# Two tiles of the first expert moved among the last operations of attention, with that expert's weights split there

## The chip, the cores and the metric

The kernel runs on one core of one Trainium2 chip. The metric is the device time of one execution in microseconds (us), the median of several runs. A core has five engines with a queue of instructions each: TensorE (PE in the rows, its weight loads PEld), VectorE (DVE), ScalarE (ACT), GpSimd (POOL) and SyncE (SP), which here issues DMAs. An engine takes its queue in order, and the queue is fixed when the kernel is built. An instruction that waits for another engine holds up everything behind it on its own engine.

## The reference

```python
def reference(q,k,v,mem_k,mem_v, moe weights, moe2 weights):   # 4 x 8 heads x 768 x 64
    for each chunk of 32 positions:                            # windowed attention, 8 memory keys
        scores = scale*q_c @ concat(mem_k, k[window]).T
        out_c  = softmax(scores) @ concat(mem_v, v[window])
    x = attention output as (3072, 512)
    # first MoE, one expert of 8 per token
    e = argmax(x @ w_gate);  g = softmax(x @ w_gate)[e] * sigmoid(x @ w_output_gate)[e]
    x = g * (relu(x @ w1[e]) @ w2[e])                          # 512 -> 1024 -> 512
    # second MoE, two experts of 8 per token, noisy logits
    return sum over the top 2 of weight * (relu(x @ w1[e]) @ w2[e])
```

With the inputs of the reference the first MoE's experts get 529, 195, 426, 381, 565, 320, 162 and 494 of the 3072 tokens (counted from the reference's own logits). In tiles of 128 tokens that is 5, 2, 4, 3, 5, 3, 2 and 4: 28 tiles, as many as `SPLIT1`, so the slots behind 28 are not run. Of the first 2304 tokens (18 row tiles of 128) 273 belong to expert 0, which is more than two tiles of it.

## The kernel before

**Attention** has 32 units: 4 batches, 2 halves, 4 pairs of heads. A unit runs S (scores, PE), max and subtraction (DVE), A (transposes, PE), exponentials (ACT), X (weights times values, PE) and the division (DVE, lines 242 to 244). After units 7, 15, 23, 27 and 31 `gating` runs for the finished row tiles (table `GATE`, three row tiles per half): it splits each row into two 16 bit halves with a scale (`parts`), stores the rows to `xrow` in DRAM, computes the logits, the expert and the rank of each token within its expert, and adds the token's place to `acc`, a histogram in PSUM, by a matmul of two one-hot tiles A and B (lines 346 to 348). `acc` says for each expert and rank which token stands there.

All of attention is given as operations with engine, estimated duration, reads and writes and a priority to a planner (`Plan`, lines 149 to 184). It simulates the engines by these estimates and emits the operation that can start first; among those within 60 ns the lowest priority number goes first. The result is a fixed order on each engine.

**Between** stands `placed` (lines 448 to 484): from `acc` and the counts in `base` it works out which tile slot holds which tokens. Line 453 reads `acc`, lines 455 to 457 get the first tile's rows early by an indirect DMA, line 476 writes the experts' first slots as integers, line 478 loads these into DVE registers, line 480 copies seven stretches of `acc` to their slots, and `rows_of` (lines 428 to 436) makes row numbers (`idx`) of all.

**The first MoE** (`moe`, lines 621 to 740) runs over the slots. For a tile: 8 groups of 12 matmuls for h (line 697), relu on ACT (hh, line 698), remainder on DVE (hl, line 699), and 24 matmuls for y (line 735). Then DVE works out a power of two scale (lines 765 to 775), ACT and DVE split y into two halves (`post`, lines 780 and 781), and SP stores the row and transposes it by DMA to x2T (`t2`) for the second MoE's logits, which PE computes two tiles later (`logits`, line 794). Weights are split into high and low halves: w1h and w2h on ACT, w1l and w2l on DVE (`first_w1`, `first_w2h`, `first_w2l`, lines 599 to 614). In the kernel before this is done behind `placed`, in memory that is opened only when attention's pools are closed. The first tile is transposed on PE (`first_trans`, lines 742 to 749), the others by DMA. The second MoE has 51 tiles.

## Time and profile before

| | us |
|---|---|
| median of 3 runs (1101.01 to 1102.67) | 1102.05 |
| the profiled execution | 1104.43 |
| its span in the trace | 1102.5 |
| PE busy | 1009.4 |
| DVE busy | 587.2 |
| ACT busy | 413.5 |
| POOL busy | 268.1 |

The profiled execution is one run and is 2.4 us above the median. Its span begins with the first instruction of the trace; all times of day in the rows are counted from there. The granted clock of PE is given as a share of full speed: 1.0 is 2.4 GHz and 0.5 is 1.2 GHz.

### The profile page before, as it was taken

The numbers are of one execution on the slowest core, as the hardware profiler recorded it, in microseconds if no ns is written. First come the engines' busy times: TensorE is split into PE (matmuls) and PEld (weight loads), VectorE is DVE, ScalarE is ACT, GpSimd is POOL, SyncE is SP. The second block draws the span as 40 slices with busy tenths as digits, with TensorE's granted clock in tenths as the row PEclk, the third lists the DMA queues.
The fourth block names the chain that finished last, engine by engine and source line by source line (L and its number), as shares of the span: only waits on it lengthen the run. The fifth ranks groups of instructions, "written<-read, shape, count | busy, mean of one in ns | idle before, by whom it ended". The sixth has DMA issues, their size and how long they took to land. (4 is left out here: it accounts for less than half of the span.)

```text
span 1102.5 us, 33444 instructions
## 1 busy us (share of the span) xinstructions
PE 1009.4 (92%) x12480; PEld 880.8 (80%) x12480; DVE 587.2 (53%) x1777; ACT 413.5 (38%) x659; POOL 268.1 (24%) x371
## 2 busy tenths in 40 slices
PE   5688839999989999898999999899999999999995
PEld 3567728888878888787888888788888888888884
DVE  3579885376577577858635225335352442525321
ACT  2568862374344365616114114124142331424010
POOL 4434111011111111110123322324233243333321
PEclk7799869999999999999999999999999999999998
DMA  8696229989596969865356537637456374563421
GB/s 324 242 397 229 85 73 260 220 256 307 113 252 148 202 192 191 244 176 141 119 115 180 167 95 150 174 89 194 139 148 192 96 221 138 155 188 84 110 70 35
DMA packets 183575, 190.47 MB, mean 173 GB/s; under 512 B 120378, under 2 KB 139066, under 8 KB 182336
## 3 DMA queue, kind: packets, MB, share of 16 engines
q1 hardware_dynamic: 167904, 139.51, 47.2%
q0 software_dynamic: 14400, 46.27, 14.1%
q8 instruction: 101, 1.65, 0.6%
q10 hardware_dynamic: 1056, 2.10, 0.5%
q14 instruction: 114, 0.93, 0.3%
HBM read 389.51 MB, written 34.53 MB: 385 GB/s over the span
## 5 line engine op out<-in xcount | busy, mean ns | idle before, releaser
L697 PE MATMUL h<-xT,w1h 128*128 128x128 f16 x4928 | 376.4, 219 | 0.0
L697 PEld LDWEIGHTS <-w1h 128*128 128x128 f16 x5056 | 309.3, 98 | 22.9 <-issue 20.7
L698 ACT ACTIVATE hh<-h 128x512 fp32r<-128x512 f32 x158 | 94.2, 597 | 529.4 <-PE h L697 500.4
L699 DVE SCALAR_TENSOR_TENSOR hl<-h,hh 128x512 fp32r<-128x512 f32 x158 | 108.7, 689 | 278.1 <-ACTq L659 180.7
L697 PE MATMUL h<-xT,w1l 128*128 128x128 f16 x2464 | 239.3, 219 | 4.9 <-DVEq L657 3.1
L697 PEld LDWEIGHTS <-w1l 128*128 128x128 f16 x2528 | 169.0, 98 | 7.4 <-DVEq L657 3.2
L933 POOL DMA_INDIRECT out_dram<-o,idxC x51 | 51.3, 1006 | 207.2 <-DVE c L920 187.0
L916 POOL DMA_INDIRECT prev<-out_dram,idxC x50 | 60.7, 1213 | 144.3 <-issue 52.8
L735 PE MATMUL y<-w2h,hl 128*128 128x512 f32 x320 | 86.8, 393 | 4.7 <-DVEq L657 2.8
L735 PE MATMUL y<-w2h,hh 128*128 128x512 f32 x320 | 85.9, 407 | 4.7 <-ACTq L657 3.0
L735 PE MATMUL z<-w2h,hh 128*128 128x512 f32 x312 | 84.4, 412 | 3.7 <-ACT hh L698 2.2
L735 PE MATMUL y<-w2l,hh 128*128 128x512 f32 x320 | 87.1, 395 | 0.0
L735 PE MATMUL z<-w2h,hl 128*128 128x512 f32 x312 | 85.7, 397 | 0.6 <-DVEq L657 0.3
L735 PE MATMUL z<-w2l,hh 128*128 128x512 f32 x312 | 84.6, 393 | 0.0
L596 DVE SCALAR_TENSOR_TENSOR w1l<-stg,wscl,w1h 128x1024 f16<-128x1024 f32 x60 | 74.3, 1279 | 11.7 <-ACT w1h L595 11.7
L614 DVE TENSOR_TENSOR w2l<-stg,w2h 128x1024 fp32r<-128x1024 f32 x64 | 75.4, 1218 | 0.3 <-ACT w2h L618 0.3
L735 PEld LDWEIGHTS y<-w2h,hl 128*128 128x128 f32 x320 | 59.7, 188 | 19.5 <-DVEq L657 3.8
L577 ACT ACTIVATE junk<-stg 128x1024 bf16<-128x1024 f32 x64 | 67.7, 1058 | 16.6 <-DMA stg<-in_w_dram 6.6
L735 PEld LDWEIGHTS z<-w2h,hl 128*128 128x128 f32 x312 | 59.4, 191 | 15.0 <-DVEq L657 1.9
L735 PEld LDWEIGHTS y<-w2l,hh 128*128 128x128 f32 x320 | 60.5, 189 | 13.3
L735 PEld LDWEIGHTS y<-w2h,hh 128*128 128x128 f32 x320 | 55.6, 188 | 19.0 <-ACTq L657 6.0
L618 ACT ACTIVATE w2h<-stg 128x1024 fp32r<-128x1024 f32 x60 | 60.0, 1049 | 28.3 <-PE h L697 14.4
(280 smaller groups left out, 1164.4 us busy)
## 6 DMA issues: line engine op xcount, KB each, us to landing
stg<-in_w_dram SPq DMA_DIRECT2D x312, 1024.0 KB
vx<-in_v_dram SPq DMA_DIRECT2D x8, 1560.0 KB
x<-row SPq DMA_DIRECT2D x26, 256.0 KB
xrow<-rows SPq DMA_DIRECT2D x8, 792.0 KB
out_dram<-zero SPq DMA_DIRECT2D x8, 768.0 KB
qs<-in_q_dram SPq DMA_DIRECT2D x7, 768.0 KB
kk<-in_k_dram SPq DMA_DIRECT2D x4, 800.0 KB
kk<-in_k_dram SPq DMA_DIRECT2D x3, 784.0 KB
```

Source lines behind the costliest of these rows:

```text
L577: for k in range(4): tc.nc.scalar.activation(g.junk,g.stg1[k//2][:,k%2],AF.Abs,accum_out=g.wscl[:,5+k:6+k])
L596: if 1 in parts: nc.vector.scalar_tensor_tensor(l[:,f:f+2],w,g.wscl[:,4:5],h[:,f:f+2],op0=ALU.mult,op1=ALU.subtract)
L614: tc.nc.vector.tensor_tensor(g.w2l[f],quarter(g,f),g.w2h[f],op=ALU.subtract)
L618: tc.nc.scalar.activation(g.w2h[f],quarter(g,f),AF.Copy)
L697: nc.tensor.matmul(o,w[i][:,k,fi%4*128:fi%4*128+128],xt[:,l*4+k],start=n==0,stop=n==11); n+=1
L698: nc.scalar.activation(hh[i],ph[i],AF.Relu)
L699: nc.vector.scalar_tensor_tensor(hl[i],ph[i],0.0,hh[i],op0=ALU.max,op1=ALU.subtract)
L735: for k in range(4): nc.tensor.matmul(py,x[h][:,k],w[2*h+k//2][:,k%2],start=i==0 and k==0,stop=i==5 and k==3)
L916: nc.gpsimd.indirect_dma_start(out=pv[s%2],out_offset=None,in_=out,in_offset=bass.IndirectOffsetOnAxis(ap=ic[s][:,0:1],axis=0), bounds_che ...
L933: nc.gpsimd.indirect_dma_start(out=out,out_offset=bass.IndirectOffsetOnAxis(ap=ic.pop(s)[:,0:1],axis=0),in_=o,in_offset=None, bounds_check ...
```

## The change

`Q1=2` tiles of expert 0 leave the loop over slots and become operations of attention's planner.

- `places`, after unit 23: raises expert 0's count to at least 256, reads the first two columns of `acc` (so only the tokens of the 18 row tiles counted by then), makes their row numbers and gathers both tiles' rows.
- `weights`: splits expert 0's weights with priorities 38 to 40, and loads the second expert's weights after that. Their memory is a pool that takes the place of buffers of attention (`early1`: q, k, v and row buffers of one parity; `early3`: qbd and e), closed as soon as the last units no longer use them.
- `early(t)`: a whole tile with priority 44 or 46, in attention's PSUM tiles A, S and X: 8 transposes, copy, h, hh and hl, y, scales, the split, store and transposing DMA.
- `placed` no longer fetches a first tile. The loop begins at slot 2, with `first_trans` for that slot. `post` and `t2` are not called for slots 0 and 1, the zero fills go to slots 2 to 9, and `tail` is cleared by POOL at the start instead of by DVE in `placed`. `NS1` is 33 instead of 31, and codes for flags are 8192 instead of 4096.

```diff
+    def places():
+        P({"DVE":80},lambda _: nc.vector.tensor_scalar(g.base[:,0:1],g.base[:,0:1],128.0*Q1,None,op0=ALU.max),w=["base"],prio=26.0)
+        def rows(_):
+            nc.vector.tensor_copy(pl,g.acc[:,0:Q1])
+            rows_of(nc,pl,o,idx)
+        P({"DVE":800},rows,w=["idx0"],r=["acc"],prio=26.0)
+        for i in range(Q1):
+            P({"Pool":1300},lambda _,i=i: nc.gpsimd.indirect_dma_start(out=g.x0[i],out_offset=None,in_=g.xrow[0:18*128],
...
+    def weights():
+        P({"SP":1},lambda _: g.room1(),w=["free"]+[("v",0,h) for h in range(2)]+[(a,0,p) for a in ("q","k","kx") for p in range(4)]+[("km",0)]+
+            [("xr",i,p) for i in range(2) for p in range(4)],prio=24.0)
...
+        for half in range(2):
+            for f in (0,2):
+                P({"ACT":940},lambda _,w=w,half=half,f=f: nc.scalar.activation(g.w1h[half][:,f:f+2],w,AF.Copy,scale=g.wscl[:,4:5]),w=[("w1h",half,f)],r=["free","wscl",("stg",f//2)],prio=38+half)
+                P({"DVE":1280},lambda _,w=w,half=half,f=f: nc.vector.scalar_tensor_tensor(g.w1l[half][:,f:f+2],w,g.wscl[:,4:5],g.w1h[half][:,f:f+2],op0=ALU.mult,op1=ALU.subtract),
...
+        for f in range(4):
+            P({"ACT":940},lambda _,f=f: nc.scalar.activation(g.w2h[f],quarter(g,f),AF.Copy),w=[("w2h",f)],r=["free",("stg",2+f//2)],prio=40)
+            P({"DVE":1180},lambda _,f=f: first_w2l(tc,g,f),w=[("w2l",f)],r=[("w2h",f),("stg",2+f//2)],prio=40)
...
+        for c in range(4):
+            P({"ACT":940},lambda _,c=c: nc.scalar.activation(g.junk,g.stg1[c//2][:,c%2],AF.Abs,accum_out=g.wscl[:,5+c:6+c]),w=[("scl2",c)],r=[("stg",c//2)],prio=40.0)
+    def early(t):
+        pr=44.0+2*t
+        def tr(_):
+            for j in range(8): nc.tensor.transpose(pt[:,j],xh[:,j*128:(j+1)*128],g.idh)
+        P({"PE":600},tr,w=["A"],r=[("x0",t),"consts"],prio=pr)
+        P({"ACT":1000},lambda _: nc.scalar.activation(g.xt0_[t],pt,AF.Copy),w=[("xt",t)],r=["A","free"],prio=pr)
+        for i in range(2):
+            for fi in range(4):
...
+                P({"PE":670},mm,w=[("S",i)],r=[("xt",t)]+[(w,i,f) for w in ("w1h","w1l") for f in (0,2)],prio=pr)
+            P({"ACT":600},lambda _,i=i,ph=ph: nc.scalar.activation(hh(i),ph,AF.Relu),w=[("hh",i)],r=[("S",i),"freex"],prio=pr)
+            P({"DVE":660},lambda _,i=i,ph=ph: nc.vector.scalar_tensor_tensor(hl(i),ph,0.0,hh(i),op0=ALU.max,op1=ALU.subtract),w=[("hl",i)],r=[("S",i),("hh",i)],prio=pr)
...
+            P({"PE":930},mm,w=[("X",t)],r=[(("hh","hl")[a],h)]+[(("w2h","w2l")[w],2*h+j) for j in range(2)],prio=pr)
...
+        P({"DVE":1150},scales,w=[("c0",t)],r=[("X",t),("x0",t),"winv"],prio=pr)
...
+        P({"SP":2000},store,r=[("r2",t,0),("r2",t,1)],prio=pr)
...
+        if n==23: places()
...
+    weights()
+    for t in range(Q1): early(t)
     P.run()
...
-    if x0 is not None:
-        o=rt.tile([128,4,1],F32,name="plc0",bufs=1); idx=rt.tile([128,1],I32,name="idx0",bufs=1)
-        rows_of(nc,pl[:,0:1],o,idx)
-        nc.gpsimd.indirect_dma_start(out=x0,out_offset=None,in_=rows,in_offset=bass.IndirectOffsetOnAxis(ap=idx[:,0:1],axis=0))
...
+    if s0==Q1: XT[s0]=first_trans(tc,g,XG[s0])
+    for s in range(s0,s0+2): trans(s)
+    if s0==Q1: tab=tab()
...
-    run(0,SPLIT1,hook_last,tab)
+    run(Q1,SPLIT1,hook_last,tab)
...
-    first_w1(tc,g); first_w2h(tc,g)
-    for f in range(2): first_w2l(tc,g,f)
-    stage1(tc,g,g.w1[1:2])
```

The planner's choices show in the order of instructions. First VectorE where the low halves of w1 are made. Before, all four stand behind `placed`, in a row with the clearing of `tail`:

```order
474 L1003 MEMSET tail 128x496
475 L1004 COPY tail<-plc_2551 128x31 [waits DVE_49]
476 L1011 MEMSET base 128x8
477 L605 SCALAR_TENSOR_TENSOR w1l_2587<-stg_68,wscl,w1h_2585 128x1024 [waits DMAHW6_49,DMAHW5_49,DMAHW7_49,DMAHW4_49,Activation_49]
478 L605 SCALAR_TENSOR_TENSOR w1l_2587<-stg_69,wscl,w1h_2585 128x1024 [waits Activation_49]
```

Now the first of them stands between steps of units 27 and 28 (S, m, e and xr are a unit's tiles, s its sums); three more follow in the next 17 rows and the four of w2 in the 42 after those:

```order
352 L228 MEMSET S_148 64x8 [waits PE_49]
353 L229 TENSOR_REDUCE m_136<-S_148 128x6 [waits DVE_49]
354 L246 TENSOR_SCALAR s_139<-X_152 128x6 [waits PE_49]
355 L385 SCALAR_TENSOR_TENSOR w1l_2082<-stg_68,wscl,w1h_2080 128x1024 [waits DMAHW5_49,DMAHW6_49,DMAHW4_49,DMAHW7_49,DMAHW3_49,Activation_49]
356 L247 RECIPROCAL s_139<-s_139 128x6 [waits DVE_49]
357 L231 TENSOR_TENSOR e_130<-S_148,m_136 128x384 [waits PE_49]
358 L248 TENSOR_TENSOR xr_134<-X_152,s_139 128x3x128 [waits DVE_49]
```

All eight, 9 microseconds and more of copies, have thus moved from behind the last A of `acc` to ahead of it. Second, VectorE from the last A to `placed`. Before, `placed` follows at once:

```order
432 L347 TENSOR_SCALAR B<-io_164,cl_295,code 128x192
433 L346 TENSOR_SCALAR A<-io_163,rm_294 128x128
434 L453 CAST pl<-acc 128x24 [waits PE_49]
435 L431 CAST plc_2506<-pl 128x1 [waits DVE_49]
436 L432 TENSOR_SCALAR plc_2506<-plc_2506 128x1 [waits DVE_49]
```

Now the last A is row 454, and between it and `placed` (row 475, line 535) stand the rest of tile 0 and, below, the end of tile 1 (X_152 is its y, c_317 its scale, xt_2093 its split row):

```order
466 L417 SCALAR_TENSOR_TENSOR h_2341<-S_149,h_2339 128x512 [waits Activation_49]
467 L427 TENSOR_TENSOR c_317<-x_76,winv 128x1 [waits DMASW1_49]
468 L428 TENSOR_REDUCE c_317<-X_152 128x1 [waits PE_49]
469 L429 TENSOR_SCALAR c_317<-c_317 128x1 [waits DVE_49]
470 L430 TENSOR_SCALAR c_317<-c_317 128x1 [waits DVE_49]
471 L431 TENSOR_SCALAR tail<-c_317 128x1 [waits DVE_49]
472 L432 RECIPROCAL c_317<-tail 128x1 [waits DVE_49]
473 L433 TENSOR_TENSOR c_317<-c_317 128x1 [waits DVE_49]
474 L436 SCALAR_TENSOR_TENSOR xt_2093<-X_152,c_317,xt_2093 128x512 [waits Activation_49]
475 L535 CAST pl<-acc 128x24
476 L538 TENSOR_SCALAR ci<-base 128x8
```

What followed the last A directly now stands behind a wait for PE (row 468) and one for ACT (row 474). Third, PE at the same place. Before, the last matmul of `acc` is followed by the transposes of the first tile:

```order
421 L348 LDWEIGHTS A [waits DVE_49]
422 L348 MATMUL acc<-B,A 128x192
423 L348 LDWEIGHTS A [waits DVE_49]
424 L348 MATMUL acc<-B,A 128x192
425 L746 LDWEIGHTS x_75 [waits DVE_49,DMASW0_49]
```

Now y matmuls of tile 0 (L421) stand among those of `acc`, and the first h group of tile 1 (S_148, from xt_2093) follows:

```order
657 L352 MATMUL acc<-B,A 128x192
658 L421 MATMUL X_151<-w2h_2086,h_2341 128x512 [waits DVE_49]
659 L421 MATMUL X_151<-w2h_2086,h_2341 128x512
660 L421 MATMUL X_151<-w2h_2087,h_2341 128x512 x2
661 L352 LDWEIGHTS A
662 L352 MATMUL acc<-B,A 128x192
663 L414 LDWEIGHTS w1h_2080
664 L414 MATMUL S_148<-xt_2093,w1h_2080 128x128
665 L414 LDWEIGHTS w1h_2080
```

Behind it come 4 matmuls of tile 0's y, the other 7 groups of tile 1 and the 24 matmuls of its y (up to row 872); the next PE work is the transposes of slot 2 (row 874), which wait for its gather. So of the two tiles only tile 0, but for these 4, stands ahead of the last `acc`.

## Rows read from the trace of the kernel before

**Rows 1.** The page, busy time, share of the span and instructions of each engine.

```profile
PE 1009.4 (92%) x12480; PEld 880.8 (80%) x12480; DVE 587.2 (53%) x1777; ACT 413.5 (38%) x659; POOL 268.1 (24%) x371
```

**Rows 2.** Windows: stretch, length, busy time by engine, granted clock, DMA share, GB/s.

```profile
74.93:153.72 78.79, 62.72 (x1574) 51.02 (x1569) 72.72 (x312) 62.31 (x132) 19.42 (x48) 0.90 0.45 162
...
139.40:153.72 14.32, 6.15 (x126) 3.61 (x126) 13.55 (x77) 11.53 (x23) 0.00 (x0) 0.70 0.22 84
...
153.87:160.24 6.37, 0.00 (x0) 0.00 (x1) 3.70 (x26) 4.08 (x5) 1.76 (x3) 0.50 0.32 105
160.24:168.60 8.36, 6.21 (x56) 5.63 (x57) 8.14 (x17) 1.02 (x1) 4.26 (x5) 0.50 0.33 79
...
179.04:190.01 10.97, 10.97 (x121) 9.72 (x121) 3.85 (x10) 1.88 (x3) 2.36 (x4) 1.00 1.12 183
190.01:203.67 13.66, 11.45 (x133) 10.09 (x133) 4.12 (x11) 6.48 (x11) 1.58 (x3) 1.00 1.06 247
203.67:214.96 11.29, 11.29 (x134) 10.03 (x133) 4.81 (x16) 1.88 (x3) 1.17 (x2) 1.00 1.17 217
```

**Rows 3.** Waits of VectorE, 74.93 to 153.72: total us, times, longest.

```profile
DVE rk L331 <- PE gate L313: 2.2, 1, 2.2
DVE S L224 <- PE S L220: 0.8, 3, 0.4
```

**Rows 4.** Groups by line, 153.87 to 179.04: busy us, mean ns, idle before.

```profile
L605 DVE SCALAR_TENSOR_TENSOR w1l<-stg,wscl,w1h 128x1024 f16<-128x1024 f32 x4 | 4.9, 1280 | 0.0
L614 DVE TENSOR_TENSOR w2l<-stg,w2h 128x1024 fp32r<-128x1024 f32 x4 | 4.8, 1217 | 0.0
L577 ACT ACTIVATE junk<-stg 128x1024 bf16<-128x1024 f32 x4 | 4.2, 1058 | 0.1
L611 ACT ACTIVATE w2h<-stg 128x1024 fp32r<-128x1024 f32 x4 | 3.9, 1041 | 0.0
L699 DVE SCALAR_TENSOR_TENSOR hl<-h,hh 128x512 fp32r<-128x512 f32 x2 | 1.4, 688 | 1.9 <-ACT hh L698 1.9
```

**Rows 5.** Timeline from the last A to the first h: start, us, instruction, idle before.

```profile
153.18 0.25 DVE L346 TENSOR_SCALAR A<-io,rm 128x128 f16<-128x128 bf16 x1
...
153.87 0.18 DVE L453 CAST pl<-acc 128x24 f16<-128x24 f32 x1 [0.44 <-PE acc L348]
...
156.71 1.30 POOL L457 DMA_INDIRECT x<-xrow,idx  x1 [18.94 <-DVE si L476]
...
158.60 1.50 DVE L480 CAST pl<-acc 128x24 f32 x7 [2.08 <-issue]
...
160.24 1.03 PE L746 MATMUL T<-idh,x 128*128 128x128 f16 x8 [6.41 <-DMA x<-xrow,idx]
...
161.00 0.18 DVE L435 CAST idx<-plc 128x31 int32<-128x31 f32 x1
...
161.50 1.02 ACT L748 ACTIVATE xTe<-T 128x1024 f16<-128x1024 f16 x1 [3.56 <-DVE s1c L1001]
...
162.63 1.01 PE L697 MATMUL h<-xTe,w1h 128*128 128x128 f16 x8 [1.35 <-issue]
```

**Rows 6.** Waits of PE, 150 to 215: total us, times, longest.

```profile
PE lgpk L794 <- DMA x2T<-row: 2.2, 1, 2.2
```

**Rows 7.** Timeline of PE, tile 1 at full clock: first h group, first y.

```profile
179.04 0.62 PE L697 MATMUL h<-xT,w1h 128*128 128x128 f16 x8
...
184.38 2.12 PE L735 MATMUL z<-w2h,hh 128*128 128x512 f32 x8
```

**Rows 8.** Timeline behind tile 1's y: scale, then its split on ACT and VectorE.

```profile
190.21 0.69 DVE L765 TENSOR_REDUCE sc<-z 128x1 f32<-128x512 f32 x1 [3.97 <-PE z L735]
...
191.75 0.16 DVE L775 TENSOR_TENSOR sc<-sc,c 128x1 f32<-128x1 f32 x1
...
193.62 0.69 ACT L780 ACTIVATE row<-z,sc 128x512 f16<-128x512 f32 x1
194.69 0.75 DVE L781 SCALAR_TENSOR_TENSOR row<-z,sc,row 128x512 f16<-128x512 f32 x1 [0.47 <-DVEq L685]
```

More of the change, by code (lines that the diff above doesn't have):

```diff
@@ L661, in moe @@
         for s in range(s0,s0+3): gather(s)
[L662 to L669 removed]
+    if s0==Q1: XT[s0]=first_trans(tc,g,XG[s0])
+    for s in range(s0,s0+2): trans(s)
+    if s0==Q1: tab=tab()
+    if s0 and (not taken or s0==Q1):
+        regs(s0-1)
+        if s0==Q1:
+            with tc.If(R[s0-1].scale>0): w1_scale(tc,g)
+        split(s0-1,0); split(s0-1,1)
+        if not second: restage(s0-1)
+    if not early: regs(s0)
     bgn=lambda s: 40 if s<early else BGN+(s>=20)
@@ L704, in moe @@
                 if i==1 and not last: split(s,0)
-            if s==0 and not early: first_w2l(tc,g,2+i)
             if s==0 and early and i==0: split_w2(tc,g,1)
@@ L712, in moe @@
             w1_mags(tc,g); w1_allmags(tc,g)
-            if not early: scale()
         hook(s,2)
@@ L997, in two_moe_kernel @@
         r={}
[L998 removed]
+        run_all(placed(tc,g,NS1,Q1,r))
         g.st1,g.si1,g.idx1,g.valid1,ix=r["s"],r["si"],r["idx"],r["v"],r["ix"]
```

129 lines of the change are left out of this document (82 added, 47 removed).

## The prediction

> **What bounds the kernel now.** I read the page's busy times first: PE works 92% of the span, VectorE 53% [rows 1]. That average hides the place of the change, so I read the windows by stage [rows 2]. Inside the loop over tiles PE is busy 10.97 of 10.97 us and 11.29 of 11.29 us: a tile costs what PE needs. In the last part of attention it is another engine. From 74.93 (where the orders of the two kernels first part on VectorE) to 153.72, VectorE is busy 72.72 of 78.79 us, PE 62.72, ACT 62.31; in the last 14.32 us VectorE has 13.55 and PE 6.15. So the end of attention is bound by VectorE. Its listed waits there are few: one of 2.2 us for the logits on PE, and 0.8 us in three pieces [rows 3].
>
> Between the two stages lies a gap. The last A ends at 153.43, `placed` reads `acc` at 153.87, the first tile's gather starts at 156.71, PE gets its rows at 160.24 after 6.41 us of waiting, and the first h matmul is at 162.63 [rows 5]. PE does nothing there, its granted clock is 0.50, and it stays 0.50 until 168.60 [rows 2]. Tile 2 then takes 13.66 us instead of some 11.3, because a logit waits 2.2 us for x2T [rows 2, 6].
>
> I compare the moment at which tile 3 starts. Before it is 203.67 [rows 2]. From there on both kernels run the same tiles on a PE that is the bound, so a shift of that moment is a shift of the end.
>
> **The last A.** What moves ahead of it on VectorE: four w1l at 1.280, together 4.9 us, and four w2l at 1.217, together 4.8 [rows 4]; one hl at 0.69; the early places, seven small instructions like those from 153.87 on and the maximum on the counts, some 1.3 with the copy for the inverse scale. Sum 11.7 us. Nothing leaves VectorE ahead of the last A: the units, the gatings and the histogram are all still there, only in another order (units 27 to 31 now stand behind the histogram of row tiles 12 to 17). VectorE has no cover for this work, being the bound itself. Its idle time is 78.79 - 72.72 = 6.07 us [rows 2].
>
> - If all of this idle time is filled, the last A ends at 153.43 + 11.7 - 6.07 = 159.1.
> - If none is, at 165.1.
> - If the in-order queues add waits (ACT gets eight weight copies among the last exponentials, about 1.04 us each [rows 4], and PE's y matmuls stand ahead of the counts that VectorE waits for), later; I allow 3 us, 168.1.
>
> In the last 14 us, where w2l lies, only 0.77 us is idle, and most of the rest is small gaps between dependent instructions, which new instructions have too. The one large wait, 2.2 us, could take a copy. I take 164.5, a little below the case in which the idle time stays, since rows 2 show it so full.
>
> **From the last A to PE's end of tile 1.** PE in order: VectorE's hl of tile 0's second half behind the A, 0.85 with its passage; four y of tile 0, 0.93; the last `acc`, 0.2; one h group, 0.66; four more y, 0.93; seven h groups, 4.65; 24 y. A tile at full clock has 8 groups in 184.38 - 179.04 = 5.34 us [rows 7], 0.66 each, and its y until VectorE begins to read it at 190.21 [rows 8], 5.8. With 0.15 for gaps this is 14.2 us. The clock should be 1.00 here, since PE has tile 0 to work on before.
>
> **From there to the first h of slot 2.** VectorE's queue holds `placed` behind tile 1's end: the scales, 190.21 to 191.91, take 1.70 [rows 8], with their start after y 1.76; the ACT half 0.69 and the VectorE half 0.75 [rows 8], 3.4 in all with passages. Then `placed` as before: from 153.87 to the first copy at 158.60 [rows 5] 4.73 us, less the seven early place instructions that left (about 1.0), plus one for the least count; copies 1.50; row numbers, the last needed at 161.00 + 0.18. That is 6.6, so the gather starts at 10.0 behind PE's end. From the gather's start to its rows it was 160.24 - 156.71 = 3.53 us; transposes 1.03, copy 1.02 [rows 5], 0.1 more for passage. Together 15.85 us. Before, the way from the last `acc` (read at 153.87) to the first h at 162.63 took 8.8 us: then the first tile's numbers came from one short chain, now they come behind seven copies and a register load of 2.08 [rows 5], and behind tile 1.
>
> The Trainium skill ("DMA: Bandwidth & Descriptors", section "Anatomy of one DMA — SWDGE (gpsimd) path") gives such a transfer about 2.0 us plus its bytes over 436 GB/s. For the 270 KB of a gathered tile this is an estimate of 2.6 us, and the forecast would be 0.9 us lower by it. The trace's 3.53 contains POOL's 1.30 of issuing, and I use the trace.
>
> **Slot 2.** 5.34 + 5.8 and a logit, 11.3, without the wait of 2.2, since tile 0's x2T is stored long before. But PE has been idle for 13.7 us. After 6.41 us of waiting the clock was 0.50 from 160.24 to 168.60 [rows 2, 5], of which 162.63 to 168.60 was matmuls: 5.97 us at half speed, 3.0 lost. I take 2.9, as some of it was waiting. Bounds: 0 if the clock stays up, 4.2 if the whole 8.36 us is work.
>
> **The sum.** Tile 3 starts at the last A + 14.2 + 15.85 + 11.3 + 2.9 = last A + 44.25. With 164.5 that is 208.75, against 203.67: +5.1 us. The profiled execution's 1104.43 would become 1109.5; it is 2.4 above the median, so on the median 1102.05 + 5.1 = **1107.2**. In words: one tile of 11 us leaves PE's path, and two things use it up: 11.7 us of VectorE work on the path that ended attention, which used to run beside PE's first tile, and a gap of 15.85 instead of 8.8.
>
> Costed at nothing: the second expert's loads (SP, DMA share 0.22 in the last part), its four magnitudes on ACT (4.2 us [rows 4], behind the last attention work, ACT being free from there), two more zero fills, clearing `tail` on POOL at the start (0.5 us, beside the first loads). If POOL's clearing delayed the first unit it would add up to 0.6. Tile count and slots are the same, 28; if padding made a 29th tile it would be 11.3 us more, but expert 0 has 273 tokens in the first 18 row tiles, so it does not.
>
> **Rivals.**
>
> *Faster, the clock.* The granted clock is 0.70 in the last 14 us, while PE has 6.15 us of work, and 0.50 behind [rows 2]. With tile 0's matmuls between, PE may keep full clock to the end of attention and across the gap. Then VectorE's waits for PE (3.0 us [rows 3]) shrink and the 2.9 us go too. All idle time (6.07) and the 2.9 together are 9.0 us; the last A at 165.1 without either gives +5.7 with the 2.9. It decides from 7.9 us of these 9.0: then the time is under 1099.85, at best 1102.05 + 5.7 - 9.0 = 1098.8. Against it: PE idle for 6.41 us had 0.50 behind it, and now it idles twice as long.
>
> *Same.* The copies are free to slip between the units' waits, the last A is at 159.1 to 161.5, and the gap stays: -0.3 to +2.1, about 1103. For it: they are fillers of lowest priority. Against it: only 3.0 of the 6.07 us are waits that could take a copy of 1.2.
>
> *Slower still, the queues.* ACT holds eight weight copies in pairs among the last exponentials, each pair 2.1 us [rows 4], and VectorE's low halves wait for them. If units 28 to 31 stop at this, the last A is at 168 or later and tile 1's x2T or the loads for the second expert come late as well: +8.7 or more, 1111.
>
> **How the numbers follow.** A measurement of this kernel can tell about 0.2%, 2.2 us. My forecast, 1104.3 to 1109.8, has 0.53; slower still 0.12; the same 0.22; faster 0.13. So slower 0.65, same 0.22, faster 0.13. The range leaves out half of the faster case's chance and a little above slower still: 1099.5 to 1112.
>
> **What would show it.** The last A of line 350 between 163 and 166, VectorE idle 5 us or more on the way from 74.93; PE's last y of tile 1 some 14 us later; POOL's gather of slot 2 10 us behind that, PE idle 13 to 14 us before the transposes, clock 0.50 after; slot 2's y without a wait on x2T; tile 3 at 208.75. I am wrong if the last A comes by 161, if `placed` or PE's next work does not wait for tile 1, or if tiles later in the loop gain or lose.

## The result, and the profile after

| | before | after |
|---|---|---|
| median, both on one chip, us (lowest to highest of 4) | 1101.53 (1097.63 to 1102.67) | 1114.41 (1113.09 to 1116.32) |
| the profiled execution | 1104.43 | 1113.95 |
| its span | 1102.5 | 1112.2 |
| start of tile 3 (slot 3, counted from 0) | 203.67 | 214.16 |

The ratio is 1.0128, with an interval of 1.0108 to 1.0147: the changed kernel is 14 us slower. I had forecast +5.1 us and 1099.5 to 1112. The sign is right, the size is not, and the range does not hold the time.

Between the two profiled executions the difference is 9.5 us (9.7 in span), and it is all there when tile 3 starts: +10.5. From there to the end it takes 898.8 us before and 898.0 after. So whatever this pair of traces can show lies ahead of 214.16. (Over all fourteen traces of this document, the way from tile 3 to the end takes 893.6 to 906.6 us.) The page's busy times say nothing of it:

```profile
PE 1010.5 (91%) x12496; PEld 881.3 (79%) x12496; DVE 586.5 (53%) x1779; ACT 414.9 (37%) x660; POOL 268.1 (24%) x372
```

Against [rows 1] no engine moves by more than 1.4 us in 1112. The time is lost in waits. These are the windows of the changed kernel by stage (stretch, length, then busy time and count of PE, PEld, DVE, ACT, POOL, granted clock, DMA share, GB/s):

```profile
75.94:166.50 90.56, 70.79 (x1670) 59.19 (x1669) 82.72 (x329) 72.75 (x146) 22.91 (x52) 0.91 0.53 185
160.00:165.00 5.00, 1.89 (x27) 1.10 (x14) 4.68 (x25) 3.55 (x8) 0.00 (x0) 0.86 0.43 156
165.00:171.00 6.00, 5.78 (x18) 3.89 (x19) 2.24 (x12) 1.20 (x3) 0.61 (x2) 0.55 0.36 135
171.00:183.00 12.00, 12.00 (x125) 10.18 (x121) 3.74 (x10) 1.88 (x3) 0.00 (x0) 1.00 0.18 45
183.00:198.97 15.97, 0.01 (x1) 0.03 (x1) 8.45 (x55) 0.69 (x1) 4.39 (x8) 0.64 0.24 61
198.97:203.94 4.97, 3.55 (x33) 3.29 (x34) 0.00 (x0) 1.02 (x1) 1.14 (x2) 0.50 0.70 184
203.94:214.16 10.22, 10.22 (x111) 9.04 (x109) 1.75 (x4) 5.69 (x10) 0.00 (x0) 0.97 0.53 131
214.16:225.43 11.27, 11.27 (x134) 10.09 (x133) 4.81 (x16) 1.98 (x5) 2.76 (x5) 1.00 0.89 213
```

The first row runs from the row sums of the first gating to the end of the last A. The same stretch of the kernel before:

```profile
74.93:153.43 78.50, 62.48 (x1573) 50.92 (x1568) 72.71 (x312) 62.02 (x132) 19.42 (x48) 0.90 0.44 161
```

Read against this and [rows 2] they give the story in four steps.

- The last A ends at 166.50. From the row sums to there VectorE is busy 82.72 of 90.56 us; before it was 72.71 of 78.50. So 10.0 us of work have come, and its idle time has not been filled but has grown from 5.79 to 7.84 (the 6.07 of the prediction runs 0.29 us beyond the A). The rest of the later A, 1.0 us, is a later start: the row sums come at 75.94 instead of 74.93.
- From 160 to 165 PE has 1.89 us of work in 5, in the next 6 us the granted clock is 0.55 on the mean, and only behind 171 is it 1.00.
- From 183.00 to 198.97 PE has 0.01 us of work: 16 us of nothing, where before it waited 6.41 [rows 5].
- Behind the gap the clock is 0.50 for 5 us, then comes back. Slot 2 ends with no wait for x2T, unlike [rows 6], and tile 3 takes 11.27, as in [rows 2] (11.29).

The timeline shows the second and third of these (start, duration, engine, line, operation, in brackets the engine's idle time before and what ended it):

```profile
165.22 2.07 PE L421 MATMUL X<-w2h,h 128*128 128x512 f32 x4 [2.30 <-DVE h L417]
166.26 0.24 DVE L350 TENSOR_SCALAR A<-io,rm 128x128 f16<-128x128 bf16 x1
167.18 2.05 PE L421 MATMUL X<-w2l,h 128*128 128x512 f32 x4
169.13 1.77 PE L421 MATMUL X<-w2h,h 128*128 128x512 f32 x4
170.74 0.26 PE L352 MATMUL acc<-B,A 128*128 128x192 f16 x1
...
181.92 1.09 PE L421 MATMUL X<-w2l,h 128*128 128x512 f32 x4
183.05 0.69 DVE L428 TENSOR_REDUCE c<-X 128x1 f32<-128x512 f32 x1 [4.26 <-PE X L421]
186.18 0.17 DVE L535 CAST pl<-acc 128x24 f16<-128x24 f32 x1
190.45 1.50 DVE L558 CAST pl<-acc 128x24 f32 x7 [2.47 <-issue]
192.86 0.18 DVE L518 CAST idx<-plc 128x33 int32<-128x33 f32 x1
193.48 0.20 POOL L1094 MEMSET apart<- 128x128 f32 x1 [26.55 <-DVE tq L582]
193.82 1.00 POOL L1095 MEMSET prev<- 128x512 f32 x2
194.77 0.33 POOL L893 COPY nz<-x 128x8 f32<-128x8 f32 x2
195.25 1.01 POOL L701 DMA_INDIRECT xg<-xrow,idx  x1 [0.15 <-issue]
198.97 1.01 PE L812 MATMUL T<-idh,xg 128*128 128x128 f16 x8 [15.96 <-DVEq L724]
201.40 1.04 PE L766 MATMUL h<-xTe,w1h 128*128 128x128 f16 x8 [1.42 <-ACTq L724]
```

PE waits for VectorE's hl until 165.22. The y matmuls of tile 0 behind that wait take 2.07, 2.05 and 1.77 us for four, where four of tile 1 take 1.09. `acc` is complete at 171.00. VectorE could read it then; it reads it at 186.18, because in its queue the end of tile 1 stands ahead, and that waits until 183.05 for PE. Only then come the slots' table, the indices at 193.04, five small pieces of work on POOL, the gather, the transposes, the copy.

For the experiments I use stretches between events of a trace, so that a kernel's start and its later tiles don't enter: "sm" is the row sums of the first gating (VectorE `sm<-ex`, 74.93 in before), A the end of the last A, E the end of PE's last y of tile 1, h the first h of slot 2, t3 the start of tile 3, which the texts written before the runs call the third tile. In us:

| | sm | sm to A | A to E | E to h | h to t3 | sm to t3 |
|---|---|---|---|---|---|---|
| before | 74.93 | 78.50 | | | | 128.74 |
| after | 75.94 | 90.56 | 16.51 | 18.39 | 12.76 | 138.22 |

### The profile page after: what moved, and what is told of

Same layout as the page of the kernel before. It is cut to its first block, busy times and chain, and to the rows that moved or that the text cites. A ratio compares the mean times of both kernels' runs of the same rounds, so it can differ in the third digit from the quotient of the medians.

```text
span 1112.2 us, 33430 instructions
## 1 busy us (share of the span) xinstructions
PE 1010.5 (91%) x12496; PEld 881.3 (79%) x12496; DVE 586.5 (53%) x1779; ACT 414.9 (37%) x660; POOL 268.1 (24%) x372
## 5 line engine op out<-in xcount | busy, mean ns | idle before, releaser
L766 PE MATMUL h<-xT,w1h 128*128 128x128 f16 x4800 | 366.5, 219 | 0.0
L766 PEld LDWEIGHTS <-w1h 128*128 128x128 f16 x4928 | 300.8, 98 | 21.7 <-issue 16.9
L767 ACT ACTIVATE hh<-h 128x512 fp32r<-128x512 f32 x154 | 91.9, 597 | 499.9 <-PE h L766 474.5
L768 DVE SCALAR_TENSOR_TENSOR hl<-h,hh 128x512 fp32r<-128x512 f32 x154 | 105.9, 689 | 278.6 <-ACTq L726 178.7
L766 PE MATMUL h<-xT,w1l 128*128 128x128 f16 x2400 | 233.1, 219 | 1.9 <-DVE winv L675 1.9
L766 PEld LDWEIGHTS <-w1l 128*128 128x128 f16 x2464 | 164.4, 98 | 3.1 <-DVE w1l L674 3.1
L801 PE MATMUL y<-w2l,hh 128*128 128x512 f32 x312 | 84.2, 392 | 0.0
L801 PE MATMUL z<-w2l,hh 128*128 128x512 f32 x304 | 82.3, 393 | 0.0
L655 ACT ACTIVATE junk<-stg 128x1024 bf16<-128x1024 f32 x60 | 63.4, 1057 | 20.7 <-DMA stg<-in_w_dram 14.3
L801 PEld LDWEIGHTS z<-w2h,hh 128*128 128x128 f32 x304 | 54.3, 193 | 17.0 <-ACTq L724 3.4
```

The costliest lines, as they stand in the source:

```text
L655: for k in range(4): tc.nc.scalar.activation(g.junk,g.stg1[k//2][:,k%2],AF.Abs,accum_out=g.wscl[:,5+k:6+k])
L766: nc.tensor.matmul(o,w[i][:,k,fi%4*128:fi%4*128+128],xt[:,l*4+k],start=n==0,stop=n==11); n+=1
L767: nc.scalar.activation(hh[i],ph[i],AF.Relu)
L768: nc.vector.scalar_tensor_tensor(hl[i],ph[i],0.0,hh[i],op0=ALU.max,op1=ALU.subtract)
L801: for k in range(4): nc.tensor.matmul(py,x[h][:,k],w[2*h+k//2][:,k%2],start=i==0 and k==0,stop=i==5 and k==3)
```

## The experiments

My theory behind the result: the loss has two parts, VectorE's added work ahead of the last A, and the slots' table behind tile 1 in VectorE's queue. The rivals: the half clock of PE behind the gap, POOL's small work ahead of the gather, the transposes at the border, and the start of the kernel. All edits are against the changed kernel; ratios are to the kernel before, timed on the same chip beside them; its own median was 1099.74, 1106.11 and 1100.54 us in the three comparisons that follow, so the times themselves should not be set side by side.

### Repeats of both kernels

The changed kernel once more, unedited:

> The changed kernel as it is, beside the kernel before on this chip. The first comparison had four runs of each (1.0128 of the time before, 1.0108 to 1.0147), and traces of kernels with the same order up to the last A differ by 2 us there, from one start to another. Theory (the loss is in the place of the change, 10 us and more): ratio 1.009 to 1.014; from the first gating's sum on VectorE (75.94 in the first trace) to the last A 90 to 93 us, from there to PE's last y of tile 1 16 to 17, from there to slot 2's first h 18 to 18.6, slot 2 12.5 to 13.5. Rival (half of the loss was that run's): ratio under 1.007, and one of these stretches 3 us shorter.

Measured: 1120.58, ratio 1.0135 (1.0108 to 1.0162). sm 78.57, sm to A 91.03, A to E 16.85, E to h 18.60, h to t3 12.89, sm to t3 139.37. The four stretches repeat to within 0.5 us each. The start to sm does not, nor does the way from t3 to the end, 906.6 us here and 898.0 in the first trace. Two kernels below (POOL's work behind the gather, PE kept busy) have the same order of instructions up to E, and their sm to A is 92.54 and 92.65. So a difference of 2 us in this stretch can be chance.

The kernel before once more, a single execution:

> The kernel before, unchanged, to see how far its own trace moves from one execution to the next. In the first trace the third tile starts 128.7 us behind the first gating's sum on VectorE, in two traces of the changed kernel 138.2 and 139.4 behind it; the difference, 9.5 to 10.6 us, is less than the 13 to 14.5 us of the timed comparisons. Theory (the first trace is of a long execution, 1104.4 us against a median of 1101.5, and the stretch is one of the places): 125 to 127 here. Rival (the rest of the loss lies ahead of this stretch or behind it): 128 to 129.5 again.

Measured: 1104.41, sm 73.64, sm to t3 131.23. So sm to t3 of before is 128.74 and 131.23, mean 130.0, and of after 138.22 and 139.37, mean 138.8: the stretch explains 8.8 us of the ratio's 14. Two more things stand outside of it. First, sm itself comes later: 74.9 and 73.6 in before, 75.0 to 79.1, mean 77, in the twelve traces of the changed kernel and its variants. Part of the cause is seen. `tail` is now cleared by POOL first of all, and POOL's first iota, behind it, comes at 8.77 instead of 8.11. The first two rows are of after, the last is of before:

```profile
0.74 0.54 POOL L1055 MEMSET tail<- 128x528 f32 x1 [0.29 <-POOLq L1125]
8.77 0.23 POOL L94 IOTA jp<- 128x128 int32 x1 [7.48 <-issue]
```

```profile
8.11 0.23 POOL L93 IOTA jp<- 128x128 int32 x1 [7.65 <-issue]
```

That is 0.66 us of some 2.8. In the other trace of before the iota comes at 8.33, in the twelve others at 8.72 to 9.55, 0.8 later on the mean. The rest stays open. Second, both profiled executions of before lie above their medians, by 2.9 and 3.9 us, while those of the twelve changed kernels lie between 3.7 below and 5.7 above, 0.3 above on the mean. Together with the start this would account for the rest of the 14 us, but two executions don't show that a profile slows one kernel and not the other. The stretch and the start make 11.6 us of the 14.1 and 14.9 that the two comparisons give; 2.5 to 3.3 us stay unplaced.

### The table ahead of the early tiles

`placed` becomes one operation of the planner, with a priority ahead of the early tiles, and the gather of slot 2 another one, into a buffer of its own:

```diff
+        gen=placed(tc,g,NS1,Q1,g.res)
+        P({"DVE":8300},lambda _: run_all(gen),w=["slots"],r=["acc","base"],prio=43.0)
+        P({"Pool":1300},lambda _: nc.gpsimd.indirect_dma_start(out=g.xs,...
...
-        r={}
-        run_all(placed(tc,g,NS1,Q1,r))
```

> The changed kernel with the slot table made directly behind the last A: it becomes an operation of the planner with priority 43, ahead of tile 1's end, and slot 2's rows are gathered there into a buffer of their own. Nothing else changes. Theory (of the 29 us between PE's last y of tile 1 and the third tile, 16 are PE waiting for a table that stands behind tile 1 on VectorE): the table is done some 8 us after the last A, near 174.5, the rows are there near 178.5, before PE ends tile 1 near 182 to 183; slot 2's first h follows 2 to 6 us behind that instead of 18.4, tile 3 starts at 196 to 200 instead of 214.2, the time is 1097 to 1101, so below the kernel before or level with it. Rival (the loss is VectorE's load ahead of the last A and the clock, and the order behind it only moves the wait): PE's gap stays above 12 us and the time above 1110.

Measured: 1098.35, ratio 0.9973 (0.9945 to 1.0000). The same kernel once more, beside later ones:

> The kernel with the slot table ahead of tile 1's end once more, beside the next one on the same chip, since chips differ (the kernel before had medians of 1099.7 and 1106.1 us in the last two calls). First result 0.9973 of the time before (0.9945 to 1.0). Theory: 0.994 to 1.001, the third tile 125 to 126 us behind the first gating's sum. Rival (the planner's other order that came with the earlier transposes, and not the chip, made the next kernel slower): the same ratio here and a clearly larger one for the kernel with transposes and tables in the planner.

Measured: 1099.66, ratio 1.0000 (0.9981 to 1.0018). The timeline of the first of the two:

```profile
164.37 0.24 DVE L350 TENSOR_SCALAR A<-io,rm 128x128 f16<-128x128 bf16 x1
...
165.94 0.17 DVE L541 CAST pl<-acc 128x24 f16<-128x24 f32 x1
172.80 0.18 DVE L524 CAST idx<-plc 128x33 int32<-128x33 f32 x1
174.22 1.01 POOL L459 DMA_INDIRECT xs<-xrow,idx  x1 [10.40 <-DMA xrow<-rows]
185.30 0.91 PE L818 MATMUL T<-idh,xs 128*128 128x128 f16 x8 [3.40 <-DVE s1c L1092]
188.85 1.03 PE L772 MATMUL h<-xTe,w1h 128*128 128x128 f16 x8 [2.65 <-ACTq L730]
```

`acc` is read 1.3 us behind the last A instead of 19.7, the gather starts at 174.22 and is hidden behind tile 1. E to h is 6.95 and 6.96 instead of 18.39 and 18.60, sm to t3 125.4 and 127.8 instead of 138.8. The whole loss is regained, nearly all of it in E to h: from sm to E it takes 105.5 and 107.3 us, in after and its repeat 107.1 and 107.9. Of all that can be undone alone, the place of the table is the largest part: 11.5 us of gap. What is left of the gap is two waits at the border, 3.40 for VectorE's copy of the table, and 2.65 for ACT, of which 1.0 is its copy of the transposed rows and the rest is put down by the profile to its queue.

### POOL's work behind the gather

The clearing of `apart` and `prev` and the two copies to nz move behind the first gathers:

```diff
+        if s==Q1 and place==-1:
+            nc.gpsimd.memset(g.apart2,0.0)
+            for t in g.pv: nc.gpsimd.memset(t,0.0)
+            for i in range(Q1): nc.gpsimd.tensor_copy(g.nz[:,i],g.x0[i][:,513:521])
...
-    for i in range(Q1): nc.gpsimd.tensor_copy(g.nz[:,i],g.x0[i][:,513:521])
```

> The changed kernel with one thing moved: on POOL the four fills and copies that stand ahead of slot 2's gather (one of 128x128, two of 128x512, two copies of 8 columns) are put behind the first four gathers. In the trace of the changed kernel slot 2's row numbers are written at 193.04 and the gather starts at 195.25, with 193.48 to 195.1 spent on these fills. Theory (POOL's queue, which the prediction left out, is one of the terms): the gather starts at 193.1 to 193.5, tile 3 starts at 212 instead of 214.16, the time falls by 1.8 to 2.2 us against the changed kernel's 1114.4. Rival (the gather waits for memory of attention to come free, which ends with VectorE's work at 193.3, and for its own start): no move beyond 0.3 us.

Measured: 1112.32, ratio 1.0106 (1.0045 to 1.0168). E to h 17.37, 1.0 less than after. The rows of this kernel:

```profile
196.88 0.18 DVE L518 CAST idx<-plc 128x33 int32<-128x33 f32 x1
...
198.14 1.01 POOL L701 DMA_INDIRECT xg<-xrow,idx  x1 [27.26 <-DVE tq L587]
```

POOL is free, and still the gather starts 1.08 us behind the indices (2.21 in after). The profile names a small VectorE operation of the due-time table as what released it. So of the 2.2 us only 1.1 belonged to POOL's queue. The rest is another wait, which I did not take apart. On the whole nothing is gained that can be told from chance: sm to t3 is 139.79, no less than in after, and the interval of the ratio holds after's 1.0128.

### The low halves of w2 behind the histogram

They get `acc` among their reads, so that the planner can't put them ahead of the last A:

```diff
-... first_w2l(tc,g,f),w=[("w2l",f)],r=[("w2h",f),("stg",2+f//2)],prio=40)
+... first_w2l(tc,g,f),w=[("w2l",f)],r=[("w2h",f),("stg",2+f//2),"acc"],prio=40)
```

> The changed kernel with the four w2l copies (4.9 us of VectorE) made to wait for the whole histogram, so that they stand behind the last A; PE has tile 1's h groups (5.3 us) to cover them. Theory (VectorE's load sets the last A): the last A ends 4 to 5 us sooner, at 161.5 to 162.5 instead of 166.5, and tile 3 starts 3 to 6 us sooner, 208 to 211. Rival (the last A is held by waits on PE and ACT, 7.9 us of idle time on VectorE, and copies only fill it): the last A moves by less than 1.5 us and the time does not fall.

Measured: 1106.63, ratio 1.0062 (1.0026 to 1.0099), against 1.0128 and 1.0135 of after. sm to A 88.70, A to E 12.92, E to h 18.81, h to t3 14.13, sm to t3 134.56, 4.2 less than after. Two things gained. The 4.8 us of copies behind the A brought the A forward by 1.9 and 2.3 us against after and its repeat. And A to E fell by 3.6 and 3.9: PE had other tile work while VectorE finished the histogram, and its clock stayed up. One thing lost: slot 2 took 1.2 to 1.4 us longer, as the half clock behind the gap lasted longer there (0.52 on the mean for the first 6.3 us). The gain ahead of the A is no larger than the spread of that stretch above; the one behind it is. Windows of this kernel, to be compared with the second and third row of after above:

```profile
160.00:165.00 5.00, 4.76 (x60) 3.86 (x57) 4.67 (x28) 4.94 (x11) 0.00 (x0) 1.00 0.04 12
165.00:171.00 6.00, 6.00 (x74) 5.41 (x72) 5.84 (x10) 1.68 (x3) 1.06 (x2) 1.00 0.71 199
```

PE is busy 4.76 of 5 us instead of 1.89, and has 1.00 where after has 0.55. VectorE's load ahead of the last A is the second part of the loss, and of the price of these four copies more is paid between A and E, in PE's wait and clock, than in the A itself.

### PE kept busy across the gap

Fifty matmuls, whose result nothing uses, ahead of the transposes of slot 2:

```diff
+    if s0==Q1:
+        d=g.psum.tile([128,512],F32,name="y",bufs=1)
+        for _ in range(50): nc.tensor.matmul(d,g.junk[:,0:128],g.junk[:,0:512],start=True,stop=True)
+        XT[s0]=first_trans(tc,g,XG[s0])
```

> The changed kernel with 50 matmuls on a tile of zeros (10.7 us at full clock) put into PE's gap between tile 1's y and slot 2's transposes; their results are not used. It prices the clock of slot 2 alone. Theory: the granted clock is 1.0 when slot 2's h begins, where it is 0.50 for 2.9 us in the changed kernel; slot 2 takes 11.3 instead of 12.76 us and the time falls by 1.3 to 1.5 us. Rival (the clock falls again in the 3 us to the transposes, or the matmuls end late and push these): no gain, up to 1 us slower.

Measured: 1120.54, ratio 1.0178 (1.0123 to 1.0232). The rows of the dummy matmuls, and the window of slot 2:

```profile
196.18 0.59 PE L731 MATMUL y<-junk 128*128 128x512 bf16 x1 [9.09 <-DVE pl L558]
196.99 12.33 PE L731 MATMUL y<-junk 128*128 128x512 bf16 x48 [0.22 <-issue]
```

```profile
211.19:222.46 11.27, 11.27 (x133) 10.09 (x133) 1.75 (x4) 5.70 (x10) 0.00 (x0) 1.00 0.47 119
```

They did not start when PE came free: by the profile they waited 9.09 us for VectorE's copies out of `acc`, most likely because their PSUM tile takes over attention's memory. So they ran at the wrong time, ended at 209 and pushed slot 2's h (E to h 24.10). As a way to gain it failed, as a measurement it worked: slot 2 at full clock is 11.27 us, in after 12.76. So the half clock behind the gap costs 1.5 us in after. In other traces slot 2 took 12.89 (the repeat), 13.31 (POOL's work behind the gather) and 14.13 (w2's low halves later) behind a gap of 15 to 16 us, so its price goes up to 2.9. As the cause of the 14 us it is ruled out.

### w2's low halves on POOL

```diff
-            P({"DVE":1180},lambda _,f=f: first_w2l(tc,g,f),...
+            P({"Pool":2400},lambda _,f=f: nc.gpsimd.tensor_tensor(g.w2l[f],quarter(g,f),g.w2h[f],op=ALU.subtract),...
```

> The changed kernel with the four w2l subtractions (4.9 us) on POOL instead of VectorE. No trace so far has this form on POOL; its fill of 128x512 takes 0.5 us, its copy of 64x384 0.53, so 1 to 3 us each. POOL is idle from 139.7 to 166.3. Theory (VectorE's load sets the last A): the last A comes 3 to 5 us sooner, 86 to 88 us behind the first gating's sum instead of 90.6 to 92.6, and the time falls by 3 to 6 us. Rival (VectorE and POOL slow each other while both work, or waits hold the last A): VectorE's instructions of the same form get longer, the last A moves by less than 1.5 us.

Measured: 1121.10, ratio 1.0144 (1.0112 to 1.0176); sm to A 94.22, longer than after's 90.56 and 91.03, though 4.8 us of VectorE's work are gone, and the ratio is no better than after's. The timeline says why. POOL's row first, then two of VectorE's:

```profile
145.03 6.97 POOL L391 TENSOR_TENSOR w2l<-stg,w2h 128x1024 fp32r<-128x1024 f32 x3
```

```profile
136.97 1.28 DVE L385 SCALAR_TENSOR_TENSOR w1l<-stg,wscl,w1h 128x1024 f16<-128x1024 f32 x1
...
144.56 8.53 DVE L385 SCALAR_TENSOR_TENSOR w1l<-stg,wscl,w1h 128x1024 f16<-128x1024 f32 x1
```

The same VectorE instruction takes 1.28 us alone and 8.53 when three of POOL's run beside it: it ends at 153.09, 1.1 us behind the last of them, and it got in at neither of the two borders between them (147.36 and 149.66). It did not share, it stood still.

### Slot 2's transposes early as well

The table as above, and slot 2's transposes and their copy as planner operations too (priority 47), so that the loop begins with h at once:

```diff
+        P({"PE":600},tr,w=["A"],r=["xs","consts"],prio=47.0)
+        P({"ACT":1000},lambda _: nc.scalar.activation(g.xts,pt,AF.Copy),w=["xts"],r=["A"],prio=47.0)
...
-    if s0==Q1: XT[s0]=first_trans(tc,g,XG[s0])
+    if s0==Q1: XT[s0]=g.xts
```

> The kernel with the slot table ahead of tile 1's end, and slot 2's transposes and copy also made operations of the planner (priority 47, tile A of attention). With the table alone 6.95 us were left between PE's last y of tile 1 and slot 2's first h: 3.4 of waiting for the transposes, which waited for memory that VectorE still used, then transposes, copy and passage. Theory: the transposes run during tile 1's y, the first h still waits for attention's PSUM (VectorE and ACT read tile 1's y for some 3.4 us), so 3.4 to 4.5 us are left, and the time is 2 to 3.5 us under that kernel's 1098.4, 0.994 to 0.996 of the kernel before. Rival (registers, branches and queues at the border of the loop hold slot 2, not the transposes): the 7 us stay.

Measured: 1111.35, ratio 1.0048 (1.0019 to 1.0076). sm to A 81.95, A to E 24.19, E to h 7.49, sm to t3 127.79. E to h did not fall below the 6.95 of the table alone, so it is not the rows that PE waits for at the border. The profile names no releaser here (issue); the due-time table is ready 1.2 us before the first h, and that it and the registers loaded from it hold PE is borne out below, where the table comes early too. The lines of this kernel:

```profile
187.15 0.34 DVE L637 CAST tab<-to 33x6 int32<-33x6 f32 x1
188.67 1.03 PE L779 MATMUL h<-xts,w1h 128*128 128x128 f16 x8 [7.49 <-issue]
```

The planner also moved three of w2's four low halves behind the last A here, by its own choice. Against the table alone sm to A is 6.2 us less and A to E 6.9 more.

The same with w2's low halves on POOL:

> The table ahead of tile 1's end, slot 2's transposes in the planner, and w2l on POOL, all three. Theory (the three losses add up: VectorE's load, the table behind tile 1, the border): 0.987 to 0.992 of the time before, 1087 to 1092; the last A 84 to 88 us behind the first gating's sum, slot 2's first h 20 to 23 us behind the last A instead of 35. Rival (with the table on VectorE directly behind the last A, tile 1's low halves wait for it, so that PE's y is late and takes back what the last A gives): 0.994 or more.

Measured: 1113.78, ratio 1.0069 (1.0040 to 1.0098). sm to A 86.55, 4.6 longer than without POOL's part, though VectorE has one subtraction less there. Three of POOL's subtractions run from 142.93 on for 8.15 us. That row first, then VectorE's timeline beside it:

```profile
142.93 8.15 POOL L391 TENSOR_TENSOR w2l<-stg,w2h 128x1024 fp32r<-128x1024 f32 x3 [6.84 <-ACT at L238]
```

```profile
144.59 0.56 DVE L248 TENSOR_TENSOR xr<-X,s 128x384 f32<-128x384 f32 x1
...
145.97 2.90 DVE L301 SCALAR_TENSOR_TENSOR rows<-xr,sc,rows 128x512 f16<-128x512 f32 x1
148.80 2.31 DVE L326 SCALAR_TENSOR_TENSOR k<-d,rev 128x24 f32<-128x24 f32 x1
151.04 0.74 DVE L301 SCALAR_TENSOR_TENSOR rows<-xr,sc,rows 128x512 f16<-128x512 f32 x1
```

`k<-d,rev` works on 24 values and takes 2.31 us (0.15 to 0.18 without POOL beside it), `rows<-xr,sc,rows` takes 2.90 in the first row and 0.74 in the next, when POOL is done. `xr<-X,s`, which has one input in PSUM, keeps its 0.56. So VectorE waits where both of its inputs lie in SBUF, until a POOL instruction has ended. The Trainium skill says so ("SBUF — State Buffer", sections "Who interferes with whom" and "Summary: rules for kernel authors"): a VectorE instruction with two inputs in SBUF contends with a GpSimd instruction that reads SBUF, and the one that comes second is blocked until the first has ended. These rows agree: POOL's three begin at 142.93, 145.97 and 148.28, the last ends at 151.08, and `k<-d,rev` ends at 151.11, with 2.16 us lost on an instruction of 0.15. Which of the two came first is less clear in the kernel of "w2's low halves on POOL": there VectorE's row begins 0.5 us ahead of POOL's (144.56 and 145.03), and it still ends behind all three.

### The due-time table early as well

On top of the last but one (w2's low halves on VectorE), the due-time table becomes a planner operation too:

```diff
+    def table(_):
+        g.st1=g.consts.tile([128,9],F32,name="s1c")
+        nc.vector.tensor_copy(g.st1,g.res["s"])
+        g.tab1=tables(tc,g,g.st1,NS1,0)
+    P({"DVE":3000},table,w=["table"],r=["slots","due"],prio=45.0)
```

> The slot table ahead of tile 1's end, slot 2's transposes in the planner, and the loop's table of due times too (3 us of small VectorE operations, priority 45, and its integer copy kept in other memory). With the transposes alone PE still idled 7.5 us between tile 1's y and slot 2's h, behind this table (done 6 us after PE's last y) and the register loads from it on each engine. Theory: the registers are loaded sooner, 3 to 5 us remain, the third tile starts 121 to 124 us behind the first gating's sum, ratio 0.990 to 0.997. Rival (the branches and register loads at the loop's border take this time whenever they start): 7 us again and no gain on the kernel beside it.

Measured: 1101.25, ratio 1.0007 (0.9984 to 1.0029). E to h is 3.45, the shortest of all, but A to E is 26.34, as VectorE now does three of w2's subtractions, `placed` and the table ahead of tile 1's hl; sm to t3 125.83. The ratio is lower than that of the version without (1.0048), though the intervals touch, and no better than that of the table of slots alone. Of the gain that I expected (0.990 to 0.997) none came. No version that I ran is clearly faster than the kernel before.

### The weights' splitting alone

No early tiles (`Q1=0`), only the first expert's weights split inside attention, without the early load of the second expert's w2; slot 0's rows are fetched by the short chain of the kernel before:

```diff
-Q1 = 2
+Q1 = 0
...
-        if n==23: places()
...
+    if NS==NS1:
+        o=rt.tile([128,4,1],F32,name="plc0",bufs=1); idx=rt.tile([128,1],I32,name="idx0",bufs=1)
+        rows_of(nc,pl[:,0:1],o,idx)
+        nc.gpsimd.indirect_dma_start(out=g.xs,out_offset=None,in_=g.xrow,in_offset=bass.IndirectOffsetOnAxis(ap=idx[:,0:1],axis=0))
```

> One part of the change alone: the weights of expert 0 are split inside attention (and the next expert's w1 is loaded and measured there), but no tile runs early; the loop starts at slot 0 with its rows gathered by the short chain as in the kernel before. The planner puts two of the four w1l ahead of the last A's rows, and the four w2l between the last A and the slot table. Theory (every microsecond of copying on VectorE ahead of the table is one of the whole): the table comes some 9 to 10 us later, the first tile no longer waits for w1l and y (0.8 and 1.7 us), the third tile starts 134 to 137 us behind the first gating's sum against 128.7, ratio 1.004 to 1.008. Rival (the copies fill VectorE's idle time): within 0.2% of the kernel before.

Measured: 1112.45, ratio 1.0111 (1.0084 to 1.0138), more than expected; sm to A 85.16, sm to t3 134.13. The rows show how w2's low halves now stand between the A and the reading of `acc`:

```profile
160.72 0.24 DVE L350 TENSOR_SCALAR A<-io,rm 128x128 f16<-128x128 bf16 x1
160.95 4.62 DVE L682 TENSOR_TENSOR w2l<-stg,w2h 128x1024 fp32r<-128x1024 f32 x4
165.49 0.17 DVE L533 CAST pl<-acc 128x24 f16<-128x24 f32 x1
```

From the A's end to the first h it takes 13.4 us, before 9.2 [rows 5], and sm to A is 6.1 longer than the mean of before (78.50 and 79.62). The three tiles behind are 5.5 us shorter (35.59 against 41.04), which I put down, without a test, to the splits that no longer run beside them. So splitting the weights early, without any early tile, makes sm to t3 4.1 us longer. The ratio says 12 us, and the profiled execution, 1110.87, is 6.5 above that of before: the part that I can't place is largest here, so how much of the whole loss the splits are by themselves, 4 us or more, stays open. That they lose and do not gain is shown by both. The splits were hidden beside PE's first tiles; inside attention they are on the path.

## Why the prediction was wrong in size

**The steps that failed** are three terms of the sum: VectorE's idle time on the way to the last A, which I let shrink and which grew; PE's clock between the last A and the end of tile 1, which I put at 1.00 and which fell to 0.55; and the start of slot 2's gather, which I put directly behind the indices. The start of the kernel, put at nothing, and some 3 us that no trace places come on top.

**Its frame held.** VectorE bounds the end of attention, tile 3's start carries the whole shift that this pair of traces shows (+10.5 there, +9.7 in span), the tiles behind it neither gain nor lose in this pair (898.8 and 898.0). Tile count 28, slot 2 without a wait for x2T, the 24 y of tile 1 at full clock: all as said. On the traces the miss is 214.16 - 208.75 = 5.4 us, in these terms:

| term | forecast | measured | off |
|---|---|---|---|
| last A | 164.5 | 166.50 | +2.0 |
| A to E | 14.2 | 16.51 | +2.3 |
| E to h | 15.85 | 18.39 | +2.5 |
| slot 2 | 14.2 | 12.76 | -1.4 |

**The last A.** I forecast 11.7 us of added work on VectorE and took 164.5 because I let 0.6 of the idle time be filled. Measured from the row sums on, it is 10.0 us of work and 2.05 us more idle time, and the row sums come 1.0 later. So the work was 1.7 too much, and the idle time grew. One of the waits of VectorE from 74.93 on, in after (total us, times, longest):

```profile
DVE lg L320 <- PE gate L317: 1.8, 2, 1.6
```

This one is not in [rows 3]. It ends at 160.18: VectorE waits for logits, and in PE's queue an h group and four y matmuls of tile 0 (158.55, 1.18 us) stand ahead of them. So tile 0 did not only fill idle time, it also made some. Of my three cases, "none is filled" (165.1) came nearest, in part by luck, as too much work and too little idle time offset each other.

**A to E.** The term that failed is "the clock should be 1.00 here". I argued that PE has tile 0 to work on. It has, but in its fixed order the y of tile 0 waits for an hl that VectorE reaches only at 164.50, between steps of the histogram. So PE idled 3 of 5 us, and three groups of four y came behind it at 0.55 of the clock: 5.9 us, against 1.1 to 1.2 for each group elsewhere in this trace (1.09 at 181.92). Four traces have the same order of instructions up to E, and the clock came back at a different moment in each, soonest in "PE kept busy":

```profile
170.30 2.07 PE L421 MATMUL X<-w2h,h 128*128 128x512 f32 x4 [2.30 <-DVE h L417]
172.27 1.66 PE L421 MATMUL X<-w2l,h 128*128 128x512 f32 x4
173.81 1.17 PE L421 MATMUL X<-w2h,h 128*128 128x512 f32 x4
```

| | the three groups of y | A to E | the rest |
|---|---|---|---|
| after | 5.89 | 16.51 | 10.62 |
| its repeat | 6.18 | 16.85 | 10.67 |
| POOL's work behind the gather | 6.00 | 16.57 | 10.57 |
| PE kept busy | 4.90 | 15.50 | 10.60 |

The rest is the same to 0.1 us. With three groups at 1.17 A to E would be 14.1, with the forecast at 14.2; so by these four traces the whole miss of this term is the clock. With w2's low halves out of the way PE had other work there, the clock stayed at 1.00 and A to E was 12.92.

**E to h.** VectorE's chain was sized exactly: indices at 10.03 us behind E, forecast 10.0. But I let the gather start with them. It started 2.2 us later, because five pieces of POOL's work and a wait for VectorE stand ahead of it, and I had not read POOL's queue at this place. Before, the gather of the first tile was issued early within `placed`, so the same clearing cost nothing there. The transfer then took 3.72 us, forecast 3.53; the estimate of 2.6 by the Trainium skill's formula ("DMA: Bandwidth & Descriptors", section "Anatomy of one DMA — SWDGE (gpsimd) path") is short by 1.1, and 1.01 of the 3.72 is POOL's issuing instruction. Transposes and copy with their passages took 2.43 for 2.15. My own terms add up to 10.0 + 3.53 + 2.15 = 15.68 and not to 15.85, so the miss of this term is really 2.7.

**Slot 2.** In this trace the half clock cost 1.5 us, forecast 2.9 (12.76 against 11.27 with the clock held up). PE comes back to full speed between 204 and 205, some 3 us behind the first h, sooner than in [rows 2]. In the other traces slot 2 took up to 14.13, so that this term gave 1.4 us back was luck of the one trace, and without it the miss would be nearer to 7.

**Outside the sum.** I put the sum on the median and so treated the start as equal. sm came 1.0 us later in the profiled execution (it stands in the last A above) and some 2.8 on the mean. I had bounded POOL's clearing by 0.6, and it is 0.66 where it can be seen, but I took it at nothing. The last 2.5 to 3.3 us of the ratio are not placed. No experiment tested the start, nor the second expert's loads, with which the DMA share on the way to the last A is 0.53 instead of 0.44.

**The rivals.** "Faster, the clock" was ruled out by the clock's fall ahead of `acc`. "Same" needed filled idle time and is ruled out by its growth. "Slower still, the queues" is nearest in time (1111), but for another reason: the waits that the traces show are those of PE, VectorE and POOL, each holding in a fixed queue what another waits for. ACT's copies among the exponentials have at most a small part: on the way to the last A no listed wait of VectorE is for ACT, and PE's waits for ACT's exponentials grew from 3.9 us to 4.7 (5.2 in the repeat). My text named the right mechanism, the table behind tile 1, and priced it well but for POOL. What I did not ask is what PE's wait for VectorE ahead of the last `acc` would do to its clock.

## What to carry to other kernels

When work is moved ahead into a stage, ask which engine bounds that stage: here 10 us of VectorE's work, most of it copies, left a place where it ran beside PE's tiles for one where all of it moved the end of the stage. A short chain that the next stage needs (counts, indices, gather) belongs ahead of filler work in every queue that it passes, that of the engine that issues the gather included; putting it there gave back the whole loss. And price a moved tile by the gap that it leaves at the border, not by the tile: two tiles left the loop, and its next one still started 10.5 us later.
